# Flags of the first pair in two steps, and PSUM evacuations moved from VectorE to ScalarE, in a fused chunk-selecting attention and mixture-of-experts kernel

## The chip, the cores and the metric

The kernel runs on one core of a Trainium2 chip. The metric is the device time in microseconds of one execution; the time before is the median of 3 runs. All positions in the trace are microseconds from the start of the profiled span, which is 256.9 us long.

## The reference, cut to what matters

The first half is attention over 4 batches of 8 heads, 768 positions and head size 64. Keys are grouped in 24 chunks of 32. For every query an upper bound of its score with each chunk is formed, the six best chunks within the causal range are kept, and a softmax over the kept, causal keys gives the output.

```python
k_min = np.min(k_chunks, axis=3); k_max = np.max(k_chunks, axis=3)
ub = np.sum(np.maximum(q[:, :, :, None, :] * k_min[:, :, None, :, :],
                       q[:, :, :, None, :] * k_max[:, :, None, :, :]), axis=-1)
top_chunks = np.argsort(np.where(causal, ub, -1e9), axis=-1)[..., -top_k:]
scores = np.where(sel & (pos[:, None] >= pos[None, :]), scale * q @ k.T, -1e9)
x = softmax(scores) @ v
```

The second half takes the 3072 rows of x (512 wide) through a dense two-layer network with a relu and adds the output of one of eight experts, chosen per row by the largest of eight gate logits and scaled by its softmax probability.

## The kernel before, in words

The 32 heads are worked on as 16 **pairs** of heads (`NP`), four pairs to a batch (`HP`). A pair goes through three stages.

*Preparation* of pair p. GpSimd casts k and q to fp16 (`cast_qk`, L468 and L470). `prep_k` transposes k on TensorE into PSUM (L481), ScalarE copies it out as `kp` (L483), VectorE reduces it to chunk minima and maxima (L497 to L501). `prep_q` transposes q (L513); ScalarE takes its relu `qp` (L516) and VectorE its negative (L517). `prep_kt` copies the two heads' keys into the stationary operands `kT` (L505, L506). `prep_ub` forms the upper bounds in one PSUM tile on TensorE (L523, L527); VectorE finds the eight largest of each row block with ten MAX8 instructions (L533) and compares all bounds with the sixth (L535), which gives the **flags**: 1 for a chunk that is not kept. `prep_s` transposes the six blocks of flags (L541) into a PSUM tile and copies it into rows 64 to 127 of `r0` (L544, VectorE) and rows 0 to 63 of `r1` (L545, ScalarE for the first pair, VectorE for the others). r0 and r1 are the moving operands of the two heads: 64 rows of q and 64 rows of flags.

`expand(i)` writes, on ScalarE, the large constant that multiplies the flags into `kT` buffer i (L144, L145), so that scores of dropped chunks vanish in the exponential. There are three such buffers, used in turn, and each is filled once.

*Scores and values.* A pair's work is cut into 11 **units** of 3 or 4 blocks of 128 by 128. `scores(p, u)` multiplies kT by r0 or r1 (L554), ScalarE takes the exponential `ex` (L558), GpSimd clears what lies above the diagonal in the units that hold diagonal blocks (L560), `av` multiplies by the values (L573), and `norm` (L582, L584) divides into x, held for a whole batch in `xbig`. The first unit needs only columns 0 to 511 of r0; the second needs columns up to 639.

*Fills.* While the pairs of batches 1 to 3 run, the dense network, the gate and the routing of the batch before are slipped in between the units. They begin with `xtr`: six blocks of x are transposed (L257) and copied out as `xT` (L258, VectorE). All fills share one PSUM bank while attention runs. The fills of the last batch, and the experts' 28 blocks of rows, come after the attention.

Instructions are traced in the order of the functions at the end of the kernel, but an engine's queue does not follow it: the program's builder places on each engine what is ready first, and trace order decides among what is ready together. `tc.issue_after(x)` puts what is traced inside it, as far as it runs on x's engine, behind x in that engine's queue; it is no wait for x's result. The main loop runs two units ahead (`ahead_n`) with `scores`, and puts the flags' transposes of pair p+1 into unit 2 of pair p and the preparation of pair p+2 into units 4 to 9.

Of the kernel before, what the change touches and what calls it, by code (L numbers as in the profile page):

```python
# [11 lines left out]
AF = mybir.ActivationFunctionType  # L12
ALU = mybir.AluOpType
# [4 lines left out]
def kernel(  # L18
# [12 lines left out]
    nc = tc.nc  # L31
    B, H, S, D = q.shape
    NT = S // 128
    NC = S // 32
# [6 lines left out]
    HP = H // 2  # L41
    NP = B * HP
# [34 lines left out]
    st = [dict() for _ in range(NP)]  # L77

    def load(p, names="kqv"):
        if p >= NP:  # L80
            return
        b, hp = divmod(p, HP)
        for nm, src in (("k", k), ("q", q), ("v", v)):
            if nm not in names:
                continue
            f = aload.tile([128, 2, NT, D], FP, name=nm + "f")
            st[p][nm] = f
            for g in range(2):
# [9 lines left out]
    ident = const.tile([128, 128], HF)  # L98
# [44 lines left out]
    def expand(i):  # L143
        nc.scalar.copy(kT[i][0][64:96, :], exf[0:32])  # L144
        nc.scalar.copy(kT[i][1][0:32, :], exf[0:32])  # L145
# [74 lines left out]
    NU = len(units)  # L220
# [18 lines left out]
    latest = {}  # L239
# [8 lines left out]
    def batch_fills(b):  # L248
# [4 lines left out]
        def xtr(mi):  # L253
            def f():
                tp = ptile("tr", [128, NK, 128], HF, "tp")
                for ko in range(NK):
                    nc.tensor.transpose(tp[:, ko], xbig[b % 2][:, mi, ko * 128 : (ko + 1) * 128], ident)  # L257
                nc.vector.tensor_copy(xT[:, :, mi * 128 : (mi + 1) * 128], tp)  # L258
            return f

        def gate():
# [193 lines left out]
    with (  # L455
# [21 lines left out]
        def prep_k(p):  # L477
            s = st[p]
            pk = pprep.tile([128, S], HF, name="pp")
            for t in range(NT):  # L480
                nc.tensor.transpose(pk[:, t * 128 : (t + 1) * 128], s["k16"][:, t].rearrange("p g d -> p (g d)"), ident)  # L481
            s["kp"] = kp = ahead.tile([128, S], HF, name="kp")
            nc.scalar.copy(kp.rearrange("d (T p j) -> d T p j", p=128, j=NJ),  # L483
                           pk.rearrange("d (T j p) -> d T p j", p=128, j=NJ))
            ks = ahead.tile([128, 2, NC], HF, name="ks")
            if p == 0:

                pc = pk.rearrange("d (T j c w) -> d T c j w", j=NJ, c=8, w=16)
                for i, op in enumerate((ALU.max, ALU.min)):
                    nc.vector.tensor_reduce(out=ks[:, i].rearrange("d (T c) -> d T c", c=8), in_=pc, op=op,  # L490
                                            axis=mybir.AxisListType.XY)
            else:
                kc = kp.rearrange("d (c w) -> d c w", w=32)
                k1 = ahead.tile([128, 2, NC, 16], HF, name="k1")
                k2 = ahead.tile([128, 2, NC, 8], HF, name="k2")
                for i, op in enumerate((ALU.max, ALU.min)):
                    nc.vector.tensor_tensor(k1[:, i], kc[:, :, 0:16], kc[:, :, 16:32], op)  # L497
                    nc.vector.tensor_tensor(k2[:, i], k1[:, i, :, 0:8], k1[:, i, :, 8:16], op)
                    nc.vector.tensor_reduce(out=ks[:, i], in_=k2[:, i], op=op, axis=mybir.AxisListType.X)
            s["kb"] = kb = ahead.tile([128, 2, 2, NC], HF, name="kb")  # L500
            nc.vector.tensor_tensor(kb, ks.unsqueeze(2).to_broadcast([128, 2, 2, NC]), hmask, ALU.mult)  # L501

        def prep_kt(p):
            kp = st[p]["kp"]
            nc.vector.tensor_copy(kT[p % NB][0][0:64], kp[0:64])  # L505
            nc.vector.tensor_copy(kT[p % NB][1][64:128], kp[64:128])  # L506

        def prep_q(p):
# [7 lines left out]
            nc.scalar.activation(qp, pq, AF.Relu)  # L516
            nc.vector.tensor_single_scalar(r0, pq, -1.0, ALU.mult)  # L517

        def prep_ub(p):

            s = st[p]
            ub = pprep.tile([128, NT, 2, NC], FP, name="pp")
            nc.tensor.matmul(ub.rearrange("p t g c -> p (t g c)"), ident, cbias.rearrange("p t g c -> p (t g c)"),  # L523
                             start=True, stop=False, skip_group_check=True)
            for t in range(NT):
                for n, (src, j) in enumerate(((s["qp"], 0), (s["qp"], 1), (rT[p % NB][0], 1))):
                    nc.tensor.matmul(ub[:, t].rearrange("p g c -> p (g c)"), src[:, t * 128 : (t + 1) * 128],  # L527
                                     s["kb"][:, j].rearrange("p g c -> p (g c)"),
                                     start=False, stop=(n == 2), skip_group_check=True)
            m = m8[p % 2]  # L530
            for t in range(1, NT):
                for g in range(2):
                    nc.vector.max(out=m[:, t, g], in_=ub[:, t, g, 0 : 4 * t + 4])  # L533
            flags = fl[p % 2].rearrange("p t (g c) -> p t g c", g=2)[:, :, :, 0:NC]
            nc.vector.tensor_tensor(flags, ub, m[:, :, :, 5:6].to_broadcast([128, NT, 2, NC]), ALU.is_lt)  # L535

        def prep_s(p):
            s = st[p]
            ps = pprep.tile([128, S], HF, name="pp")
            for t in range(NT):  # L540
                nc.tensor.transpose(ps[:, t * 128 : (t + 1) * 128], fl[p % 2][:, t], ident)  # L541
            r0, r1 = rT[p % NB]
            nc.vector.tensor_copy(r1[64:128], r0[64:128])
            nc.vector.tensor_copy(r0[64:128], ps[64:128])  # L544
            (nc.scalar.copy if p == 0 else nc.vector.tensor_copy)(r1[0:64], ps[0:64])  # L545

        def scores(p, u):
            s = st[p]
            pc = units[u]
            sp = psc.tile([128, 512], FP, name="sp")  # L550
            o = 0
            for g, kt, a, z in pc:
                w = (z - a) * 128
                nc.tensor.matmul(sp[:, o : o + w], kT[p % NB][g][:, kt * 128 : (kt + 1) * 128],  # L554
                                 rT[p % NB][g][:, a * 128 : z * 128], start=(o == 0), stop=True, skip_group_check=True)
                o += w
            ex = aexp.tile([128, 512], HF, name="ex")
            nc.scalar.activation(ex[:, 0:o], sp[:, 0:o], AF.Exp, scale=-0.125)  # L558
            if pc[0][1] == pc[0][2]:
                latest["pool"] = nc.gpsimd.affine_select(out=ex, in_=ex, compare_op=ALU.is_ge, fill=0.0, base=0,  # L560
                                        pattern=[[0, 4], [1, 2], [2, 64]], channel_multiplier=-1)
            s["ex", u] = ex
# [38 lines left out]
        load(2, "v")  # L601
        load(3, "v")
        prep_s(0)
        prep_k(1)
        prep_q(1)
        prep_kt(1)
        cast_qk(2)
        load(4, "kq")
        expand(1)
        prep_ub(1)  # L610
        expand(2)

        wq = [(e, w) for e in range(E) for w in range(2)]
        ahead_n = 2
        LAG = 1

        def finish(p, u):
# [6 lines left out]
                    fills.clear()  # L624
                    fills.update(batch_fills(p // HP)[-1])

        seq = [(p, u) for p in range(NP) for u in range(NU)]
        for i in range(ahead_n):
            scores(*seq[i])
# [176 lines left out]
```

## Time and profile before

| | |
|---|---|
| time, median of 3 (range) | 266.76 us (265.68 to 266.89) |
| profiled span | 256.9 us |
| busy: TensorE, VectorE, ScalarE, GpSimd | 83%, 70%, 69%, 63% of the span |
| batch 0, first exponential to flags of pair 5 | 16.5 to 54.5 us |
| batches 1 to 3 of the attention | 54.5 to about 168 us |
| last dense fills and experts | about 168 to 257 us |
| one exponential of 128x512, mean | 612 ns, 144 of them |
| one copy of 64x768 flags out of PSUM: VectorE, ScalarE | 548 ns, 792 ns |
| one copy of 128x512 `xT` out of PSUM, VectorE | 416 ns, 24 of them |

The shares of the whole span are averages over three stages with different limits, so the stages have to be read one by one. A mean duration is that of one instruction [...]; on ScalarE and VectorE the next instruction may start before that, so the distance from start to start in a row of back-to-back instructions is the price that a queue pays. The row of L558, for instance, has 4 instructions in 1.96 us, 0.49 us for each.

### The profile page before, as it was taken

How to read it: one execution, taken by the hardware profiler on the slowest of the kernel's cores; microseconds unless marked ns; L12 is line 12 of the kernel's file. 1: busy time of each engine (PE TensorE's matmuls, PEld its weight loads, DVE VectorE, ACT ScalarE, POOL GpSimd, SP SyncE). 2: the span in 40 equal slices, each digit the busy share in tenths (PEclk: the TensorE clock that was granted, in tenths of full speed). 3: DMA queues.
4: the chain of work that ended last, by engine and by line, in shares of the span. 5: the costliest groups of instructions: out<-in, count | busy, mean ns of one | idle time of the engine just before them, and what ended most of it. 6: DMA issues, size and time to landing. Idle time of an engine off the chain costs nothing. (4 is left out here: it accounts for less than half of the span.)

```text
span 256.9 us, 7296 instructions
## 1 busy us (share of the span) xinstructions
PE 214.5 (83%) x2547; PEld 142.1 (55%) x2547; DVE 180.5 (70%) x617; ACT 178.5 (69%) x332; POOL 160.7 (63%) x197
## 2 busy tenths in 40 slices
PE   1388887796899798899986899979999999999960
PEld 0256566565666477656665666646555555455520
DVE  6868899999968789986799997237633344455440
ACT  2698888887679887778897877954666554555530
POOL 3746988766468475867866553510887453887671
PEclk9999999999999999999999999999999999999995
DMA  6999999999959999999999884265499999786885
GB/s 174 261 266 239 199 219 262 210 188 217 281 128 240 237 215 202 183 304 174 281 228 234 159 172 129 83 187 158 106 302 137 252 276 236 115 142 84 108 103 77
DMA packets 75109, 49.89 MB, mean 194 GB/s; under 512 B 29632, under 2 KB 68160, under 8 KB 75072
## 3 DMA queue, kind: packets, MB, share of 16 engines
q0 software_dynamic: 15216, 19.09, 46.4%
q1 hardware_dynamic: 59856, 30.33, 46.1%
q8 instruction: 21, 0.34, 0.5%
q14 instruction: 16, 0.13, 0.2%
HBM read 41.66 MB, written 18.23 MB: 233 GB/s over the span
## 5 line engine op out<-in xcount | busy, mean ns | idle before, releaser
L558 ACT ACTIVATE ex<-sp 128x512 f16<-128x512 f32 (+1 forms) x176 | 92.4, 593 | 11.1 <-PE sp L554 10.8
L554 PE MATMUL sp<-rT,kT 128*128 128x128 f16 (+3 forms) x384 | 63.2, 261 | 2.6 <-ACT ex L558 1.1
L720 POOL DMA_INDIRECT out_dram<-yo,xg x28 | 43.7, 1561 | 20.7 <-DVE yo L719 14.3
L560 POOL TENSOR_SCALAR_AFFINE_SELECT ex<-ex 128x512 f16<-128x512 f16 x48 | 32.6, 689 | 37.4 <-ACT ex L558 35.1
L573 PE MATMUL op<-v,ex 128*128 128x65 f16 x672 | 49.5, 194 | 4.4 <-POOL ex L560 2.9
L573 PEld LDWEIGHTS <-ex 128*128 128x128 f16 x672 | 37.3, 98 | 18.2 <-POOL ex L560 6.7
L368 POOL DMA_INDIRECT table<-xbig,slot x24 | 24.4, 1019 | 19.1 <-DVE nf L324 11.3
L719 DVE TENSOR_SCALAR yo<-yp,xg 128x512 f32<-128x512 f32 x28 | 21.0, 750 | 21.6 <-PE yp L716 18.6
L554 PEld LDWEIGHTS <-kT 128*128 128x128 f16 x384 | 28.3, 98 | 6.4 <-issue 4.1
L710 ACT COPY ehT<-tp 128x512 f16<-128x512 f16 x28 | 16.4, 585 | 20.5 <-PE tp L708 20.4
L699 PE MATMUL hp<-we,exT 128*128 x112 | 29.1, 379 | 1.1 <-DVE xbig L584 1.1
L716 PE MATMUL yp<-we,ehT 128*128 x112 | 28.7, 379 | 0.8 <-ACT ehT L710 0.8
L383 PE MATMUL hp<-xT,wd 128*128 128x384 f16 x128 | 26.2, 325 | 1.7 <-ACT hT L385 1.1
L392 PE MATMUL yp<-wd,hT 128*128 128x512 f16 x96 | 24.4, 379 | 0.9 <-ACT ys L395 0.4
L702 ACT ACTIVATE eh<-hp 128x512 f16<-128x512 f32 x28 | 16.7, 597 | 11.5 <-PE hp L699 11.5
L693 DVE COPY exT<-tp 128x512 f16<-128x512 f16 x28 | 11.9, 423 | 15.1 <-PE tp L691 14.3
L395 ACT COPY ys<-yp 128x512 f32<-128x512 f32 x24 | 14.3, 594 | 9.6 <-PE yp L392 6.8
L385 ACT ACTIVATE hT<-hp 128x384 f16<-128x384 f32 x32 | 15.9, 496 | 6.8 <-PE hp L383 6.5
L497 DVE TENSOR_TENSOR k<-kp 128x384 f16<-128x384 f16 x30 | 13.3, 479 | 9.1 <-ACT kp L483 9.1
L584 DVE TENSOR_TENSOR xbig<-op,rs 128x384 f16<-128x384 f32 x32 | 17.6, 550 | 0.4
L483 ACT COPY kp<-pp 128x768 f16<-128x768 f16 x16 | 12.9, 805 | 6.4 <-PE pp L481 6.4
L475 POOL CAST v<-vf 128x768 f16<-128x768 f32 x16 | 13.6, 853 | 5.3 <-DMA vf<-in_v_dram 3.3
(126 smaller groups left out, 403.1 us busy)
## 6 DMA issues: line engine op xcount, KB each, us to landing
we<-in_moe_w_dram POOLq DMA_DIRECT2D x16, 512.0 KB, 8.0
kf<-in_k_dram SPq DMA_DIRECT2D x32, 192.0 KB
qf<-in_q_dram SPq DMA_DIRECT2D x32, 192.0 KB
vf<-in_v_dram SPq DMA_DIRECT2D x32, 192.0 KB
out_dram<-ys SPq DMA_DIRECT2D x48, 128.0 KB
xg<-table SPq DMA_DIRECT2D x28, 136.0 KB
table<-zt SPq DMA_DIRECT2D x9, 136.0 KB
wd<-in_moe_w_dense_dram POOLq DMA_DIRECT2D x2, 512.0 KB
```

Source lines behind the costliest of these rows:

```text
L368: sc = nc.gpsimd.indirect_dma_start(out=table, out_offset=bass.IndirectOffsetOnAxis(ap=keep["slot"][:, t : t + 1], axis=0), in_=xbig[b % 2 ...
L383: nc.tensor.matmul(hp, wd[:, ko, j * 128 : (j + 1) * 128], xT[:, ko, g * G * 128 : (g + 1) * G * 128], start=(ko == 0), stop=(ko == NK - 1))
L392: nc.tensor.matmul(yp, hold["h"][:, j, i * 128 : (i + 1) * 128], wd[:, NK + j], start=(j == 0), stop=(j == NK - 1))
L554: nc.tensor.matmul(sp[:, o : o + w], kT[p % NB][g][:, kt * 128 : (kt + 1) * 128], rT[p % NB][g][:, a * 128 : z * 128], start=(o == 0), sto ...
L558: nc.scalar.activation(ex[:, 0:o], sp[:, 0:o], AF.Exp, scale=-0.125)
L560: latest["pool"] = nc.gpsimd.affine_select(out=ex, in_=ex, compare_op=ALU.is_ge, fill=0.0, base=0, pattern=[[0, 4], [1, 2], [2, 64]], chan ...
L573: nc.tensor.matmul(s["op", g][:, t * (D + 1) : (t + 1) * (D + 1)], ex[:, o : o + 128], v16[p % NB][:, g, kt, :], start=first, stop=(last_o ...
L584: nc.vector.tensor_tensor(xbig[b % 2][:, :, h0 : h0 + D], opv[:, :, 0:D], rs.to_broadcast([128, NT, D]), ALU.mult)
L699: nc.tensor.matmul(hp, s["xT"][:, ko], wef[:, bass.ds(offs[i] + ko * 512, 512)], start=(ko == 0), stop=(ko == NK - 1))
L716: nc.tensor.matmul(yp, s["hT"][:, j], wef[:, bass.ds(offs[i] + (NK + j) * 512, 512)], start=(j == 0), stop=(j == NK - 1))
L719: nc.vector.tensor_scalar(o, yp, s["x"][:, Dm : Dm + 2].bitcast(FP), None, ALU.mult)
L720: sc = nc.gpsimd.indirect_dma_start(out=out, out_offset=bass.IndirectOffsetOnAxis(ap=s["x"][:, Dm + 2 : Dm + 4].bitcast(mybir.dt.int32), a ...
```

## The change

It has three parts. The first pair's flags are made in two steps, blocks 0 to 3 and blocks 4 and 5, so that the first unit can begin with the first step; the two units of scores that the loop runs ahead are traced before the preparation of pair 1, and the ScalarE instructions of that preparation, with the constants of `kT` buffers 1 and 2, are queued behind the second exponential. ScalarE copies the lower half of the flags (r1) out for pairs 1 to 4 as well as for pair 0. And ScalarE copies three of the six `xT` blocks of the first three batches. The aim is to have the first exponential sooner, and to share PSUM evacuation[...].

```diff
@@ xtr
-                nc.vector.tensor_copy(xT[:, :, mi * 128 : (mi + 1) * 128], tp)
+                evac = nc.scalar.copy if b < B - 1 and mi % 2 else nc.vector.tensor_copy
+                evac(xT[:, :, mi * 128 : (mi + 1) * 128], tp)
@@ prep_ub
-            m = m8[p % 2]
-            for t in range(1, NT):
+            s["ub"] = ub
+            for a, z in steps(p):
+                select(p, a, z)
+
+        def steps(p):
+
+            return ((0, 4), (4, NT)) if p == 0 else ((0, NT),)
+
+        def select(p, a, z):
+            ub, m = st[p]["ub"], m8[p % 2]
+            for t in range(max(a, 1), z):
                 for g in range(2):
                     nc.vector.max(out=m[:, t, g], in_=ub[:, t, g, 0 : 4 * t + 4])
-            flags = fl[p % 2].rearrange("p t (g c) -> p t g c", g=2)[:, :, :, 0:NC]
-            nc.vector.tensor_tensor(flags, ub, m[:, :, :, 5:6].to_broadcast([128, NT, 2, NC]), ALU.is_lt)
+            flags = fl[p % 2].rearrange("p t (g c) -> p t g c", g=2)[:, a:z, :, 0:NC]
+            nc.vector.tensor_tensor(flags, ub[:, a:z], m[:, a:z, :, 5:6].to_broadcast([128, z - a, 2, NC]), ALU.is_lt)
@@ prep_s
-            for t in range(NT):
-                nc.tensor.transpose(ps[:, t * 128 : (t + 1) * 128], fl[p % 2][:, t], ident)
             r0, r1 = rT[p % NB]
             nc.vector.tensor_copy(r1[64:128], r0[64:128])
-            nc.vector.tensor_copy(r0[64:128], ps[64:128])
-            (nc.scalar.copy if p == 0 else nc.vector.tensor_copy)(r1[0:64], ps[0:64])
+            for a, z in steps(p):
+                for t in range(a, z):
+                    nc.tensor.transpose(ps[:, t * 128 : (t + 1) * 128], fl[p % 2][:, t], ident)
+                cols = slice(a * 128, z * 128)
+                nc.vector.tensor_copy(r0[64:128, cols], ps[64:128, cols])
+
+                (nc.scalar.copy if p <= HP else nc.vector.tensor_copy)(r1[0:64, cols], ps[0:64, cols])
@@ the order of the first pairs
         prep_s(0)
-        prep_k(1)
-        prep_q(1)
-        prep_kt(1)
-        cast_qk(2)
-        load(4, "kq")
-        expand(1)
-        prep_ub(1)
-        expand(2)
+        seq = [(p, u) for p in range(NP) for u in range(NU)]
+        ahead_n = 2
+        for i in range(ahead_n):
+            scores(*seq[i])
+        with tc.issue_after(latest["exp"].ins):
+            prep_k(1)
+            prep_q(1)
+            prep_kt(1)
+            cast_qk(2)
+            load(4, "kq")
+            expand(1)
+            prep_ub(1)
+            expand(2)
```

`latest["exp"]` is the exponential that `scores` issued last. The two scores that stood ahead of the main loop are gone from there.

More of the change, by code (lines that the diff above doesn't have):

```diff
@@ L529, in prep_ub @@
                                      start=False, stop=(n == 2), skip_group_check=True)
-            m = m8[p % 2]
-            for t in range(1, NT):
+            s["ub"] = ub
[6 more added lines that the diff above has]
+            for t in range(max(a, 1), z):
                 for g in range(2):
                     nc.vector.max(out=m[:, t, g], in_=ub[:, t, g, 0 : 4 * t + 4])
-            flags = fl[p % 2].rearrange("p t (g c) -> p t g c", g=2)[:, :, :, 0:NC]
-            nc.vector.tensor_tensor(flags, ub, m[:, :, :, 5:6].to_broadcast([128, NT, 2, NC]), ALU.is_lt)
+            flags = fl[p % 2].rearrange("p t (g c) -> p t g c", g=2)[:, a:z, :, 0:NC]
+            nc.vector.tensor_tensor(flags, ub[:, a:z], m[:, a:z, :, 5:6].to_broadcast([128, z - a, 2, NC]), ALU.is_lt)
         def prep_s(p):
-            s = st[p]
             ps = pprep.tile([128, S], HF, name="pp")
-            for t in range(NT):
-                nc.tensor.transpose(ps[:, t * 128 : (t + 1) * 128], fl[p % 2][:, t], ident)
             r0, r1 = rT[p % NB]
             nc.vector.tensor_copy(r1[64:128], r0[64:128])
-            nc.vector.tensor_copy(r0[64:128], ps[64:128])
-            (nc.scalar.copy if p == 0 else nc.vector.tensor_copy)(r1[0:64], ps[0:64])
+            for a, z in steps(p):
[4 more added lines that the diff above has]
+                (nc.scalar.copy if p <= HP else nc.vector.tensor_copy)(r1[0:64, cols], ps[0:64, cols])
         def scores(p, u):
@@ L557, in scores @@
             ex = aexp.tile([128, 512], HF, name="ex")
-            nc.scalar.activation(ex[:, 0:o], sp[:, 0:o], AF.Exp, scale=-0.125)
+            latest["exp"] = nc.scalar.activation(ex[:, 0:o], sp[:, 0:o], AF.Exp, scale=-0.125)
             if pc[0][1] == pc[0][2]:
@@ L603 @@
         prep_s(0)
-        prep_k(1)
-        prep_q(1)
-        prep_kt(1)
-        cast_qk(2)
-        load(4, "kq")
-        expand(1)
-        prep_ub(1)
-        expand(2)
+        seq = [(p, u) for p in range(NP) for u in range(NU)]
[11 more added lines that the diff above has]
+            expand(2)
         wq = [(e, w) for e in range(E) for w in range(2)]
-        ahead_n = 2
         LAG = 1
@@ L625, in finish @@
                     fills.update(batch_fills(p // HP)[-1])
-        seq = [(p, u) for p in range(NP) for u in range(NU)]
-        for i in range(ahead_n):
-            scores(*seq[i])
         for i, (p, u) in enumerate(seq):
```

## The prediction

> **What bounds the kernel now.** The chain that ended last is of no use here: it ends in one scatter and goes no further back. So I cut the span into stages and read the busy time of each engine by stage; the cuts are the starts of the flags' transposes (L541), one for each pair. Columns: length, then busy time and number of instructions of PE, PEld, DVE, ACT, POOL, the clock, DMA share and GB/s.
>
> ```profile
> 14.88:22.30 7.42, 6.73 (x77) 4.23 (x75) 5.47 (x25) 6.85 (x14) 3.71 (x6) 1.00 1.24 254
> 22.30:30.30 8.00, 6.47 (x102) 4.62 (x102) 7.54 (x27) 7.07 (x14) 6.79 (x10) 1.00 1.06 225
> 30.30:37.90 7.60, 6.32 (x104) 4.85 (x105) 6.93 (x28) 6.43 (x13) 6.51 (x22) 1.00 1.15 194
> 37.90:46.50 8.60, 6.44 (x109) 4.97 (x108) 8.31 (x29) 7.32 (x15) 7.35 (x12) 1.00 1.19 259
> 46.50:54.50 8.00, 7.03 (x128) 5.46 (x128) 7.50 (x31) 7.35 (x15) 5.82 (x9) 1.00 0.94 173
> ```
>
> The first row is pair 0: ScalarE is the fullest engine, 6.85 of 7.42 us. In the four rows after it VectorE is, with 7.54 + 6.93 + 8.31 + 7.50 = 30.28 of 32.2 us, or 94%; ScalarE follows with 28.17. The same view of the first ten microseconds of batches 1, 2 and 3, where the transposes of x fall:
>
> ```profile
> 54.50:65.20 10.70, 7.60 (x138) 5.89 (x135) 10.12 (x39) 7.42 (x15) 5.89 (x8) 1.00 1.14 230
> 94.00:104.00 10.00, 8.73 (x169) 7.38 (x167) 9.38 (x32) 8.36 (x18) 5.99 (x9) 1.00 0.96 188
> 134.00:144.00 10.00, 7.48 (x133) 6.22 (x132) 9.73 (x34) 7.38 (x15) 6.00 (x9) 1.00 1.17 236
> ```
>
> VectorE is 94 to 97% busy in each head, TensorE and ScalarE have 1.3 to 3.3 us of idle time. Who waits there is in the waits of 54 to 66 us (total, times, longest):
>
> ```profile
> POOL ex L560 <- ACT ex L558: 4.0, 3, 2.1
> ACT ex L558 <- PE sp L554: 1.7, 4, 0.8
> ...
> PE tp L257 <- DVE xT L258: 0.7, 1, 0.7
> ```
>
> GpSimd waits for exponentials, ScalarE for scores, TensorE for an evacuation by VectorE: the waits lead back to VectorE. Later in each batch (104 to 134 us) TensorE is at 88 to 94% and no engine stands out, and from 175 to 215 us TensorE is busy for 39.61 of 40 us. That last stage holds none of the changed instructions, so what the attention gains or loses should reach the end one to one.
>
> DMA is busy throughout, but after 22 us no cast of k or q waits for a load, and the one long wait for values (L475, 2.2 us) ends at 20.08. I take no load as the limit.
>
> The opening, on ScalarE's timeline (start, duration):
>
> ```profile
> 11.49 0.83 ACT L144 COPY kT<-exf 32x768 f16<-32x768 f16 x1
> 12.35 0.83 ACT L145 COPY kT<-exf 32x768 f16<-32x768 f16 x1
> 13.20 0.83 ACT L144 COPY kT<-exf 32x768 f16<-32x768 f16 x1
> 14.05 0.83 ACT L145 COPY kT<-exf 32x768 f16<-32x768 f16 x1
> 15.16 0.80 ACT L483 COPY kp<-pp 128x768 f16<-128x768 f16 x1 [0.27 <-PE pp L481]
> 15.85 0.79 ACT L545 COPY rT<-pp 64x768 f16<-64x768 f16 x1
> 16.54 0.60 ACT L558 ACTIVATE ex<-sp 128x512 f16<-128x512 f32 x1
> 17.24 0.81 ACT L516 ACTIVATE qp<-pp 128x768 f16<-128x768 f16 x1
> 17.95 1.96 ACT L558 ACTIVATE ex<-sp 128x512 f16<-128x512 f32 x4
> ```
>
> The four copies of the constant (buffers 1 and 2) run from 11.49 to 14.88, while nothing else is ready: they cost nothing. Then ScalarE is busy nearly without a gap until 22.65; the third exponential starts at 17.95 + 0.49 = 18.44, the first of pair 1 at about 24.3 (the second instruction of a row at 23.84).
>
> [...]
>
> **Part 1, the opening.** Ten MAX8 take 0.95 us from 12.19, the compare 0.46. Six tenths of the first and four sixths of the second give 0.57 + 0.31: first flags at 13.07 in place of 13.60. Four transposes instead of six (0.82 for six at the start of the kernel) take some 0.6, r0's columns 0 to 511 some 0.40 (560 ns for 768), scores 0.5: first exponential at about 14.9, 1.6 us sooner than 16.54. The second step (0.37 for four MAX8, 0.16 compare) is hidden beside these transposes[...]: second exponential at about 15.8, sooner by 2.1.
>
> Against that, the four constant copies lose their free place. They are queued behind the second exponential, are ready at once, and are traced before the third exponential. kp and the relu stood ahead of the third before, too. So after the second exponential (ends 16.3) come kp 0.69, relu 0.69 and four copies at 0.86 from start to start, 3.44: third exponential at 16.3 + 4.8 = 21.1, later by 2.7 than 18.44. Pair 0 was ScalarE's stage, so I count 2.7 us as loss there, between 0.9 (one buffer's two copies first, the others in gaps) and 3.4 (all four unhidden). VectorE, which waits 0.9 us for kp now, gets it at 17.0 instead of 15.9, but has slack of 2 us in pair 0.
>
> **Part 2, flags of pairs 1 to 4.** Four VectorE copies go: 0.57 each from start to start (23.40 to 23.97), 2.3 us. VectorE falls from 30.28 to 28.0 in the four rows. ScalarE gets four at 0.69 (15.85 to 16.54), 2.8: 28.17 + 2.8 = 30.9 by busy time. But [...] there are about five rows in a pair, so packed it is 30.9 - 4 x 0.5 = 28.9. ScalarE becomes the fuller engine by a little. At 96% filled the four pairs take 28.9 / 0.96 = 30.1 instead of 32.2: gain 2.1 us. Bounds: no gain at 90%, 3.3 at 100%. Nothing new waits for this copy but the units of head 1, the last five and a half of a pair; the exponentials queued behind it wait 0.69.
>
> **Part 3, transposes of x.** In each head VectorE loses three copies at 0.33 from start to start (59.38 to 59.71), 1.0 us; ScalarE gets three. No row shows ScalarE copying this shape from PSUM in the attention, but the experts' L710 has it at 585 ns, and the equal-sized exponential gives 0.49 in a row: 1.5 us, in a stage where ScalarE has 1.6 to 3.3 idle. VectorE stays the fullest (10.12 - 1.0 = 9.1 against 7.42 + 1.5 = 8.9 in the first). I take 0.87 of the 1.0, since ScalarE's queue can hold a copy behind an exponential and the single fill bank then stays occupied: 2.6 us for three heads, between 1.2 and 3.0.
>
> **Sum.** +2.7 - 2.1 - 2.6 = -2.0: 266.76 - 2.0 = **264.8 us**.
>
> **Rivals.**
> *ScalarE becomes the limit.* For it: it is the fullest in pair 0, and gets 3.4 + 2.8 us more in the first 40. Against it: its idle time before each row. The constants cost 3.4, batch 0 gains nothing, the heads 1.2 because copies wait behind exponentials: +2.2, 269.0 us.
> *The constants hide after all.* They are pushed between exponentials that wait for scores, and pairs 1 to 4 make up the rest. Then 0 - 2.1 - 3.0 = -5.1: 261.7 us. For it: 4.0 us of ScalarE idle in the four rows of batch 0. Against it: these gaps lie at the ends of rows, under a microsecond each.
> *All cancels.* The heads are held by the single fill bank and by scores, so that they give 1.2; the opening's 2.7 is met by 2.1: -0.6, 266.2 us. For it: TensorE at 71 to 87% in the heads.
>
> **How the numbers follow.** Forecast 0.44, constants hidden 0.20, all cancels 0.14, ScalarE the limit 0.22. The bound of 0.5% is 1.33 us, so faster is below 265.4: about three quarters of the first case with its spread of 1 us (0.35) and all of the second, and a little of the third: 0.57. Slower is above 268.1: nearly all of the last case, 0.21. The rest, 0.22, is the same. The range reaches near both outer cases: 261.4 to 268.6.
>
> **What would show it.** First exponential near 14.9; L144 and L145 in front of the third exponential, which starts near 21; pair periods of 7.5 us in batch 0 with ScalarE above 93%; heads shorter by 0.9 each with VectorE still above 90%; the last stage unchanged. The prediction is wrong if the constants land elsewhere in ScalarE's queue, if another order of the fills costs more than the evacuations save, or if flags on ScalarE delay the scores of head 1.

## The result, and the profile after

The changed kernel takes 279.02 us (median of 4 runs, 277.34 to 281.72) against 266.82 us for the kernel before on the same chip. The ratio is 1.044, with a 95% interval of 1.037 to 1.051: slower by 4.4%, or 12.2 us, where 2 us less were forecast. From chip to chip the kernel before takes 258.9 to 266.8 us, so every ratio below is to its own runs on the chip of that experiment. Times are medians of all runs; some executions are slow whatever the kernel, and the ratios and their intervals leave those out.

The same view by stages as in the prediction, of the changed kernel (length, then busy time and number of instructions of PE, PEld, DVE, ACT, POOL, then the clock, DMA share, GB/s). The cuts are again the starts of the flags' transposes, now L553; the first row begins at 15.60, within pair 0:

```profile
15.60:23.50 7.90, 4.27 (x52) 3.38 (x52) 5.26 (x23) 7.29 (x12) 1.86 (x3) 0.84 1.28 255
23.50:31.90 8.40, 7.68 (x107) 6.28 (x106) 6.07 (x27) 7.29 (x15) 4.63 (x7) 0.75 0.53 125
31.90:42.70 10.80, 7.53 (x109) 5.83 (x106) 8.70 (x28) 7.58 (x15) 7.06 (x12) 0.84 1.11 190
42.70:54.70 12.00, 8.57 (x110) 6.49 (x108) 9.58 (x27) 8.40 (x16) 8.02 (x24) 0.73 0.83 177
54.70:62.80 8.10, 6.50 (x105) 4.96 (x103) 6.91 (x27) 7.10 (x15) 5.11 (x7) 0.98 1.05 207
```

Before, the four rows of pairs 1 to 4 were 8.00, 7.60, 8.60 and 8.00 us. Now they are 8.40, 10.80, 12.00 and 8.10. ScalarE was to be above 93% in them: it is at 70% in the two longest. VectorE is at 80%. No engine is full, so the rows have become a chain of waits. VectorE even has *more* busy time in the third and fourth rows (8.70 and 9.58 us) than before (6.93 and 8.31), though a copy a pair was taken from it: its instructions last longer (two `k<-k` 2.29 us in place of 0.42, in the next section).

The heads of batches 1 to 3:

```profile
62.80:72.80 10.00, 9.28 (x172) 7.57 (x169) 9.08 (x33) 9.62 (x21) 6.63 (x10) 1.00 1.03 195
106.00:116.00 10.00, 8.40 (x162) 7.19 (x160) 8.96 (x33) 8.56 (x17) 4.59 (x7) 1.00 0.94 197
149.30:159.30 10.00, 8.18 (x154) 6.85 (x155) 8.70 (x32) 7.91 (x16) 5.13 (x8) 1.00 0.81 163
```

VectorE has come down to 87 to 91%, as it was meant to. ScalarE's timeline of the opening (start, duration):

```profile
14.72 0.60 ACT L570 ACTIVATE ex<-sp 128x512 f16<-128x512 f32 x1
15.87 0.36 ACT L557 COPY rT<-pp 64x256 f16<-64x256 f16 x1 [0.55 <-DVE rT L555]
16.52 0.60 ACT L570 ACTIVATE ex<-sp 128x512 f16<-128x512 f32 x1 [0.28 <-PE sp L566]
17.01 0.79 ACT L484 COPY kp<-pp 128x768 f16<-128x768 f16 x1
17.69 0.83 ACT L517 ACTIVATE qp<-pp 128x768 f16<-128x768 f16 x1
18.54 0.83 ACT L144 COPY kT<-exf 32x768 f16<-32x768 f16 x1
...
21.07 0.83 ACT L145 COPY kT<-exf 32x768 f16<-32x768 f16 x1
21.80 2.56 ACT L570 ACTIVATE ex<-sp 128x512 f16<-128x512 f32 x5
```

The opening went nearly as forecast: first exponential at 14.72 (forecast 14.9), the four constants ahead of the third, which starts at 21.80 (forecast 21.1). What the forecast did not follow stands in the fourth row: kp of pair 1, at 17.01 in place of 15.16.

The waits of 31.9 to 54.8 us, the two long rows:

```profile
ACT ex L570 <- PE sp L566: 6.0, 4, 2.5
PE pp L528 <- DVE kb L502: 4.9, 2, 2.8
```

Before, 30.3 to 46.5 us had 2.1 and 1.2 us for these two (L558 for scores, L527 for `kb`). ScalarE now waits for scores, and scores stand in TensorE's queue behind the bounds of the next pair, which wait for `kb`, the end of VectorE's reduction of k.

Where the time lies along the kernel, read from the last `norm` of each batch in the traces (another profiled run of the kernel before has the same ends to within 0.2 us):

| length of batch, us | 0 (from the start) | 1 | 2 | 3 | end of attention |
|---|---|---|---|---|---|
| before | 52.6 | 41.7 | 42.2 | 36.3 | 172.8 |
| after | 62.8 | 43.4 | 43.5 | 39.4 | 189.1 |
| difference | +10.2 | +1.7 | +1.3 | +3.1 | +16.3 |

The profiled run of before was on a faster chip than its timed ones (258.92 us), and the stage after the attention takes 82.5 to 89.2 us in the traces, depending on the chip and the kernel; so ends of attention are compared between traces, and times only between runs of one chip. The attention itself seems not to depend on the chip: on one where the kernel before takes 264.77 us, batches 0 and 1 of `xT` alone took 52.4 and 41.7 us, and batches 2 and 3 of the flags alone 42.2 and 36.5, which is what they take before. What the attention lost did not come back in full as time (16.3 against 12.2 us), so the prediction's "one to one" did not hold; that difference was not followed up.

### The profile page after: what moved, and what is told of

Its sections match the earlier page's. It is cut to its first block, busy times and chain, and to the rows that moved or that the text cites. A ratio compares the mean times of both kernels' runs of the same rounds, so it can differ in the third digit from the quotient of the medians.

```text
span 275.5 us, 7295 instructions
## 1 busy us (share of the span) xinstructions
PE 220.6 (80%) x2547; PEld 147.2 (53%) x2547; DVE 184.1 (67%) x606; ACT 185.1 (67%) x346; POOL 161.8 (59%) x197
## 3 DMA queue, kind: packets, MB, share of 16 engines
q0 software_dynamic: 15216, 19.09, 43.5%
## 5 line engine op out<-in xcount | busy, mean ns | idle before, releaser
L570 ACT ACTIVATE ex<-sp 128x512 f16<-128x512 f32 (+1 forms) x176 | 94.4, 597 | 13.6 <-PE sp L566 12.0
L566 PE MATMUL sp<-rT,kT 128*128 128x128 f16 (+3 forms) x384 | 68.4, 272 | 2.4 <-ACT ex L570 1.4
L585 PE MATMUL op<-v,ex 128*128 128x65 f16 x672 | 53.9, 199 | 1.9 <-POOL ex L572 1.5
L585 PEld LDWEIGHTS <-ex 128*128 128x128 f16 x672 | 40.8, 102 | 15.3 <-POOL ex L572 3.2
L369 POOL DMA_INDIRECT table<-xbig,slot x24 | 25.0, 1040 | 21.3 <-DVE nf L325 11.3
L566 PEld LDWEIGHTS <-kT 128*128 128x128 f16 x384 | 29.6, 102 | 5.7 <-issue 3.4
L723 ACT COPY ehT<-tp 128x512 f16<-128x512 f16 x28 | 16.4, 585 | 22.1 <-PE tp L721 16.9
L498 DVE TENSOR_TENSOR k<-kp 128x384 f16<-128x384 f16 x30 | 19.8, 696 | 12.7 <-ACT kp L484 12.7
L715 ACT ACTIVATE eh<-hp 128x512 f16<-128x512 f32 x28 | 16.7, 597 | 11.3 <-PE hp L712 10.4
L528 PE MATMUL pp<-kb,qp 128*128 128x48 f16 x192 | 11.6, 189 | 11.8 <-DVE kb L502 9.3
L706 DVE COPY exT<-tp 128x512 f16<-128x512 f16 x28 | 11.8, 422 | 12.0 <-PE tp L704 8.7
L528 PEld LDWEIGHTS <-qp 128*128 128x128 f16 x192 | 10.4, 100 | 14.0 <-issue 12.2
```

Source lines behind the costliest of these rows:

```text
L369: sc = nc.gpsimd.indirect_dma_start(out=table, out_offset=bass.IndirectOffsetOnAxis(ap=keep["slot"][:, t : t + 1], axis=0), in_=xbig[b % 2 ...
L570: latest["exp"] = nc.scalar.activation(ex[:, 0:o], sp[:, 0:o], AF.Exp, scale=-0.125)
L585: nc.tensor.matmul(s["op", g][:, t * (D + 1) : (t + 1) * (D + 1)], ex[:, o : o + 128], v16[p % NB][:, g, kt, :], start=first, stop=(last_o ...
```

## What changed besides the instructions: two things that the traces show

**The preparation moved to another place in the queues.** Ordering each kernel's ScalarE queue in the trace, I counted how many exponentials of pair p-2 stand ahead of `kp` of pair p. Before, it is 10 or 11, that is all of them or all but one, for pairs 2 to 7, 11 and 15, and 7 for the others. After, it is 7 for every pair. The diff says nothing of these pairs: the builder places what is ready first, so an order can move far from an edit. By parts, the opening alone has 7, 9 and 9 for pairs 2 to 4 and the old order behind them, `xT` alone has 7 for pairs 11 and 15, and the flags alone keep the old order to within one place.

**In the new place it meets GpSimd's casts.** VectorE's timeline of pair 3's preparation, changed kernel:

```profile
33.67 1.26 DVE L498 TENSOR_TENSOR k<-kp 128x384 f16<-128x384 f16 x2 [0.63 <-ACT kp L484]
34.85 2.29 DVE L499 TENSOR_TENSOR k<-k 128x192 f16<-128x192 f16 x2
```

GpSimd's in the same stretch, and TensorE's next instruction after its matmuls at 35.01:

```profile
34.01 1.45 POOL L572 TENSOR_SCALAR_AFFINE_SELECT ex<-ex 128x512 f16<-128x512 f16 x2
35.42 0.81 POOL L469 CAST k<-kf 128x768 f16<-128x768 f32 x1
36.19 0.85 POOL L471 CAST q<-qf 128x768 f16<-128x768 f32 x1
```

```profile
38.10 0.24 PE L528 MATMUL pp<-kb,qp 128*128 128x48 f16 x2 [2.81 <-DVE kb L502]
```

The two L499 take 0.42 us for pair 1, where GpSimd is idle. Here they take 2.29, until the second cast is over, and TensorE stands for 2.81 us. The same happens for pair 4: 2.90 us, from 45.58 to 48.48, with the casts from 46.79 to 48.37. One of pair 4's two L499 alone takes 2.27 us, from within a select to the end of the second cast, so it was held over a row of GpSimd's instructions and not over one. Not every instruction is held: `tensor_reduce` between them (L500, 30 times) never took longer than 0.35 us in any of the runs, and VectorE's copies of flags out of PSUM (L555, L557) never longer than 0.56 us in the changed kernel. The traces show these times; by what VectorE is held was not shown.

To compare kernels I add up VectorE's busy time, over all pairs, of the instructions of a pair's preparation that read and write SBUF alone, without `tensor_reduce`: `k`, `kb`, and the copies `kT<-kp` and `rT<-rT`. Call it the **SBUF work**. Before it is 53.2 us (53.6 in the other profiled run), after 62.3, for the same instructions.

## The experiments

All ratios are to the kernel before on the same chip.

| kernel | time, us | ratio, 95% interval | end of attention, us | SBUF work, us |
|---|---|---|---|---|
| changed | 279.02 | 1.044 (1.037 to 1.051) | 189.1 | 62.3 |
| opening alone | 270.76 | 1.022 (1.016 to 1.027) | 180.2 | 57.3 |
| flags of pairs 1 to 4 alone | 267.62 | 1.011 (1.008 to 1.014) | 176.7 | 57.0 |
| `xT` alone | 268.23 | 1.013 (1.007 to 1.019) | 177.0 | 56.6 |
| flags and `xT` | 272.57 | 1.031 (1.023 to 1.038) | 182.6 | 63.0 |
| opening alone, constants early | 266.16 | 1.010 (1.007 to 1.013) | 176.8 | 55.5 |
| changed, constants early | 267.82 | 1.031 (1.024 to 1.038) | 182.9 | 64.5 |
| changed, casts later | 271.56 | 1.032 (1.025 to 1.039) | 182.4 | 49.6 |
| before, casts later | 261.68 | 1.010 (1.005 to 1.015) | 175.5 | 54.1 |
| `xT` alone, casts later from pair 5 | 263.20 | 1.016 (1.010 to 1.022) | 176.7 | 51.2 |

And with work left out, so that these are not candidates but measurements:

| kernel, casts and loads of k and q left out from pair 3 on | time, us | ratio, 95% interval | end of attention, us | SBUF work, us |
|---|---|---|---|---|
| before | 252.28 | 0.972 (0.962 to 0.982) | 166.2 | 46.2 |
| changed | 257.65 | 0.993 (0.990 to 0.995) | 171.8 | 46.8 |
| flags and `xT` | 256.93 | 0.989 (0.982 to 0.996) | 170.6 | 49.6 |
| `xT` alone | 253.85 | 0.980 (0.976 to 0.985) | 168.1 | 48.2 |

### The three parts one by one

Opening alone (the hunks of `prep_ub`, `prep_s` and the order of the first pairs, with `p == 0` kept for ScalarE's copy and VectorE for `xT`):

> The opening alone (part 1), flags and x copies on VectorE as before. Phase theory: the queue order has 7, 9, 9, 11 exponentials ahead of kp of pairs 2 to 5, so only the first one or two pairs meet the casts; the opening's 2 to 3 us and one collision of 2 us: 269 to 273 us. ScalarE theory: only the opening's own delay, 1.2 to 1.7 us at the flags of pairs 1 and 2: 268 to 269 us. If the opening alone is the loss: 276 us or more.

Flags alone, the kernel before with one line:

```diff
-            (nc.scalar.copy if p == 0 else nc.vector.tensor_copy)(r1[0:64], ps[0:64])
+            (nc.scalar.copy if p <= HP else nc.vector.tensor_copy)(r1[0:64], ps[0:64])
```

> Part 2 alone, the flags of pairs 1 to 4 on ScalarE. Phase theory: the order stays as in the kernel before (10 or 11 exponentials ahead of kp), so no more collisions and no idle TensorE; the prediction's sum says up to 2 us faster: 264 to 267 us. ScalarE theory: ScalarE at 28.9 of 30 us holds back exponentials in batch 0: 268 to 271 us.

`xT` alone, the kernel before with the hunk of `xtr`:

> Part 3 alone, three of six x copies on ScalarE. Phase theory: the heads of the batches get shorter by 1 us or more each, but ScalarE's queue now has 7 exponentials ahead of kp for all pairs from 8 on (pair 11 and pair 15 had 11), so the pairs after a head meet the casts more often; gain and loss nearly cancel: 265 to 270 us, with batch 0 unchanged. The prediction's sum: 264.2 us. ScalarE theory: heads not shorter, since copies wait behind exponentials: 267 to 268 us.

Flags and `xT` together:

> Parts 2 and 3 without the opening (flags in one step, constants in their free place, pair 1 prepared before the first scores). Phase theory: the loss comes from the order that the opening sets, in which the chunk reduction of pair p+2 on VectorE runs beside GpSimd's casts of k and q in batch 0; here ScalarE's queue has 10 or 11 exponentials of pair p ahead of kp of pair p+2 up to pair 7, as in the kernel before, so batch 0 keeps its time (flags of pair 5 within 1.5 us of 54.5) and the whole is 266 to 272 us. ScalarE theory: the copies given to ScalarE are the loss; then this is about as slow as the changed kernel, 276 to 279 us.

Each part by itself makes the kernel slower: by 2.2, 1.1 and 1.3%, which add up to 4.5, the loss of the whole (4.4). No part alone brings a gain, and none of the three was worth what it was costed at. They lose in different places. The opening costs 7.3 us in batch 0 (59.9 against 52.6), gives 1.7 back in batch 1 and costs 1.6 in batch 2; the flags 2.4 in batch 0 and 1.3 in batch 1; `xT` nothing in batches 0 and 1, 1.3 in batch 2 and 3.1 in batch 3.

The idea that was called phase theory, that the loss comes from the order that the opening sets, failed on the flags. Alone they keep that order, and with `xT` they keep it in batch 0, each to within one place; yet the flags of pair 5 come at 57.6 and 58.3 us in place of 54.5, and both times are just above the range that this idea gave. So batch 0 can lose time without the preparation moving.

### What the flags' copy did for VectorE

One place, around pair 2's flags, shows what became of the time of the copy that was taken from VectorE. VectorE in the kernel before:

```profile
30.83 0.56 DVE L544 COPY rT<-pp 64x768 f16<-64x768 f16 x1 [0.60 <-PE pp L541]
31.42 0.55 DVE L545 COPY rT<-pp 64x768 f16<-64x768 f16 x1
31.89 0.18 DVE L582 RECIPROCAL rs<-op 128x6 f32<-128x6 f32 x1
31.99 0.63 DVE L497 TENSOR_TENSOR k<-kp 128x384 f16<-128x384 f16 x2
```

and GpSimd:

```profile
30.15 0.83 POOL L468 CAST k<-kf 128x768 f16<-128x768 f32 x1
30.91 0.83 POOL L470 CAST q<-qf 128x768 f16<-128x768 f32 x1
```

While GpSimd casts (30.15 to 31.74), VectorE copies flags out of PSUM, and starts on k when the casts are over. With the copy gone (flags alone), VectorE and GpSimd:

```profile
29.99 0.56 DVE L544 COPY rT<-pp 64x768 f16<-64x768 f16 x1 [0.60 <-PE pp L541]
31.15 1.76 DVE L497 TENSOR_TENSOR k<-kp 128x384 f16<-128x384 f16 x2 [0.60 <-ACT kp L483]
```

```profile
30.97 0.83 POOL L468 CAST k<-kf 128x768 f16<-128x768 f32 x1
31.73 0.97 POOL L470 CAST q<-qf 128x768 f16<-128x768 f32 x1
```

k starts 0.84 us sooner, falls onto the casts and takes 1.76 us in place of 0.63: it ends at 32.91, where it ended at 32.62 before. Here the saved 0.57 us of VectorE became a wait for GpSimd. Besides, ScalarE's copy stands in its queue until VectorE is done with the same PSUM tile, and the exponentials behind it wait too. ScalarE at pair 3's flags, flags alone:

```profile
41.15 0.79 ACT L545 COPY rT<-pp 64x768 f16<-64x768 f16 x1 [1.03 <-DVE rT L544]
```

The two copies of one tile ran at the same time in none of the traces (in the changed kernel ScalarE's starts 0.03 to 0.83 us after the end of VectorE's), so an engine was changed and nothing was made parallel. That the casts are all of this part's loss is not shown: with casts and loads of k and q left out (below), flags and `xT` together are still 0.9 points slower than `xT` alone, though these two intervals overlap.

### The constants' place

In the opening alone, and then in the changed kernel, the four constant copies are traced ahead of the first scores:

```diff
+        expand(1)
+        expand(2)
         for i in range(ahead_n):
             scores(*seq[i])
...
-            expand(1)
             prep_ub(1)
-            expand(2)
```

> The opening alone, but with the four constant copies traced in front of the first scores, so that they keep their free place on ScalarE; flags and x copies on VectorE. ScalarE's queue then has 11 exponentials ahead of kp for pairs 2 to 7, as in the kernel before. If the constants are what makes the opening slow: 263 to 266 us against 270.8 with them queued behind the second exponential. If the split of the flags or the scores ahead of pair 1's preparation is what costs: 269 to 271 us.

> The changed kernel with the four constant copies traced ahead of the first scores, so that they have their free place again. The same edit brought the opening alone from 1.022 to 1.010. If the losses add up, this takes 1.044 - 0.012 = about 1.03; if the misplaced constants only start a delay that the later collisions would bring anyway, it stays at 1.04.

The misplaced constants cost 1.2 to 1.3% (1.022 to 1.010, and 1.044 to 1.031), some 3.3 us: close to the 3.44 us that they occupy ScalarE, and somewhat more than the 2.7 of the forecast. That it is the copies' own time is not shown: with them early, the opening alone also has the old order again (11 exponentials ahead of `kp` for pairs 2 to 7), and TensorE's clock is full from 19.8 us on and not from 26.8 (see the last section). With them early, the changed kernel takes as long as flags and `xT` alone, so there the rest of the opening costs nothing. But the opening alone still loses 1.0% with its constants free and its first exponential at 14.69. Its ScalarE queue (opening alone, constants early) shows why:

```profile
14.69 0.58 ACT L569 ACTIVATE ex<-sp 128x512 f16<-128x512 f32 x1
...
16.29 0.60 ACT L569 ACTIVATE ex<-sp 128x512 f16<-128x512 f32 x1 [0.28 <-PE sp L565]
16.78 0.79 ACT L483 COPY kp<-pp 128x768 f16<-128x768 f16 x1
```

kp of pair 1 is still behind the second exponential, 1.6 us later than before, and the flags of pair 1 come at 23.6 in place of 22.3. Pair 1 can't begin without them, so the first exponential's 1.8 us are lost again at the first change of pairs.

### Are the casts the cause?

First by leaving work out of the changed kernel and of the kernel before, the casts alone:

> The changed kernel without the casts of k and q from pair 3 on: those pairs use pair 2's k and q, so half of GpSimd's casts are left out; the order on TensorE and ScalarE is that of the changed kernel. Contention theory (VectorE's chunk reduction [...] is held while GpSimd casts): the reduction takes 1.2 us for every pair, the gaps of 2 to 3 us on TensorE in batch 0 and the halved clock go; 265 to 270 us, within 3 or 4 us of the kernel before without these casts. ScalarE theory (evacuations and constants on ScalarE hold exponentials back whatever GpSimd does): 276 us or more, and the distance stays at 10 us or more.

> The same omission (casts of k and q from pair 3 on) in the kernel before, as the reference for the run above. Contention theory: its reduction is held for some 5 us in all now (23.9 us of VectorE time for 15 pairs against 18 without), part of it beside other work: 260 to 264 us. ScalarE theory: 264 to 266 us, no change, since no ScalarE instruction is touched.

The changed kernel took 266.23 us, 1.007 (1.004 to 1.010), and the kernel before 265.27, 0.999 (0.994 to 1.003), so the gap nearly closed. But this pair is not a clean measurement: without casts the loads of k and q run ahead and those of v come late (in the kernel before, GpSimd waits 12.1 us for values in the profile without the casts, 3.3 with them). So the loads went too:

```diff
     def load(p, names="kqv"):
-        if p >= NP:
+        if p >= NP or names == "kq" and p > 2:
@@ cast_qk
+            if p > 2:
+                s["k16"], s["q16"] = st[p - 1]["k16"], st[p - 1]["q16"]
+                return
```

> The kernel before without the casts and without the loads of k and q from pair 3 on (those pairs use pair 2's), because leaving out the casts alone let these loads run ahead and made the values late. Contention theory: the chunk reduction takes 18 to 20 us in all instead of 23.9, values are no longer late, 258 to 263 us. ScalarE theory: 263 to 265 us.

> The changed kernel with the same omissions (no casts and no loads of k and q from pair 3 on); orders on TensorE and ScalarE as in the changed kernel. Contention theory: what is left of the 12 us is the opening's own delay, 1 to 4 us above the kernel before with the same omissions: 260 to 266 us. ScalarE theory: still 10 us or more above it.

> Parts 2 and 3 without the opening, with the same omissions. Contention theory: the two parts' gains, which the prediction put at 2.1 and 2.6 us, come out once no cast stands against VectorE: 1 to 5 us faster than the kernel before with the same omissions. ScalarE theory: as with all work kept, 8 us slower than it.

> Part 3 alone, with the casts and loads of k and q left out from pair 3 on (later pairs use pair 2's data). The kernel before with the same left out took 0.972 of before (252.3 us), parts 2 and 3 together 0.989. If part 3 lost only by collisions, this takes 0.972 or less. If something else in it costs time, the longer last batch above all, it takes 0.98 to 0.99, and batch 3 is longer by 1.5 to 2 us than in the kernel before with the same left out.

The kernel before gets 2.8% faster, the changed one by 5.1 points (1.044 to 0.993). The difference between the two falls from 12.2 us to 257.65 - 252.28 = 5.4, and the SBUF work of the two is nearly the same (46.2 and 46.8 us). So roughly half of the loss needs GpSimd's casts of k and q (or their loads, which this edit can't tell apart), and some 5 us do not; by the intervals of the two ratios the share is known only roughly.

The forecasts of the contention theory were too high for both kernels, and for flags and `xT` its forecast failed outright. They were to be 1 to 5 us faster than the kernel before with the same left out, and are 4.7 us slower; with all work kept it is 7.8. So the gains that the prediction saw in parts 2 and 3 did not lie hidden behind these casts. GpSimd's selects and its casts of v are still there, and flags and `xT` have 3.4 us more SBUF work than before even here (49.6 against 46.2), so collisions with those are not excluded. What holds the rest was not settled.

Then with all work kept, by moving the casts two units:

```diff
-            if u == 7:
+            if u == 9:
                 with tc.issue_after(latest["pool"].ins):
                     cast_qk(p + 3)
```

> The changed kernel with all work kept, but the casts of k and q traced at unit 9 instead of 7 of a pair, which puts them behind the select of the next pair's first unit in GpSimd's queue; the order on ScalarE (7 exponentials ahead of kp) stays. Contention theory: in batch 0 the casts now come after the chunk reduction, which falls from 3.7 and 4.2 us for pairs 3 and 4 to about 1.3; 267 to 273 us. ScalarE theory: 277 to 280 us, nothing else is changed. If later casts make k late: more than 280 us.

> The kernel before, with all its work, and only the casts of k and q moved from unit 9's place after unit 7 to after unit 9. Here the chain over k of most pairs runs after the last units of a pair, not in the middle. If the cause is the overlap of these casts with that chain, the same move that made the changed kernel 7 us faster must here be of no use or harmful: the chain's four instructions, 23.9 us over 15 pairs, grow to 27 or more, and the time goes up by 1 to 2%. If a later cast is better in itself (loads further ahead, GpSimd's queue), this one gets faster by 1% or more.

The same edit takes 1.2 points off the changed kernel (1.044 to 1.032; the two intervals still overlap a little) and adds 1.0 to the kernel before. (The "7 us" in the second expectation was taken across two chips; by the ratios it is 3.2.) A later cast is thus not better in itself, which fits that it matters where the preparation stands. The direction was forecast, the victim was not. The chain over k did not grow in the kernel before; another instruction was hit. Before with later casts, VectorE and GpSimd:

```profile
114.63 3.24 DVE L543 COPY rT<-rT 64x768 f16<-64x768 f16 x1
```

```profile
115.29 0.84 POOL L468 CAST k<-kf 128x768 f16<-128x768 f32 x1
116.06 0.83 POOL L470 CAST q<-qf 128x768 f16<-128x768 f32 x1
116.83 0.83 POOL L475 CAST v<-vf 128x768 f16<-128x768 f32 x1
```

A copy from SBUF to SBUF, 0.36 us in the median, is held until three casts in a row are over, and TensorE then stands for 2.61 us from 116.8 on. The SBUF work hardly rose (53.2 to 54.1), so the sum does not tell the loss: what counts is which instruction is held, and who waits for it.

### Why the heads gained nothing

`xT` alone, with the casts moved from pair 5 on:

```diff
-            if u == 7:
+            if u == (9 if p >= 5 else 7):
```

> Part 3 alone, all work kept, with the casts of k and q after unit 9 in place of 7 from pair 5 on, where part 3 lets the chain over k run early. If collisions are what ate part 3's saving, the chain falls from 28.3 to about 24 us and the time from 1.013 to between 0.995 and 1.003 of before. If TensorE over a whole batch is the limit, the chain falls and the time stays at 1.008 or more.

The SBUF work fell by 5.4 us, below that of the kernel before, and the time stayed at 1.016. So collisions are not what ate part 3's saving, or later casts cost as much again: in this kernel, too, a copy (`kT<-kp`) is held for 3.19 us by three casts in a row, at 68.97. The runs without casts and loads are cleaner. The stages of batches 1, 2 and 3, first before, then `xT` alone:

```profile
52.90:92.60 39.70, 35.67 (x518) 25.86 (x519) 33.00 (x140) 33.28 (x66) 19.73 (x27) 1.00 0.74 150
92.60:130.40 37.80, 35.82 (x528) 26.30 (x525) 31.76 (x129) 33.77 (x68) 22.01 (x30) 1.00 0.88 165
130.40:166.20 35.80, 32.55 (x441) 22.62 (x437) 24.29 (x103) 29.19 (x60) 16.98 (x22) 1.00 0.75 167
```

```profile
52.40:92.00 39.60, 35.97 (x517) 26.04 (x518) 33.31 (x137) 34.28 (x69) 19.68 (x27) 1.00 0.73 152
92.00:130.40 38.40, 36.25 (x529) 26.23 (x525) 31.02 (x126) 35.07 (x71) 21.94 (x30) 1.00 0.85 164
130.40:168.10 37.70, 32.64 (x441) 22.62 (x436) 23.68 (x100) 30.55 (x63) 17.74 (x22) 1.00 0.71 157
```

Both end batch 2 at 130.4 us. TensorE is busy for 90, 95 and 91% of the three stages of the kernel before: over a whole batch it is the fullest engine, and shifting VectorE's copies to ScalarE takes nothing from it. That this is what holds a batch is argued from these shares and was not tested by itself. In the heads the saving is there. With all work kept, the pair periods of the heads fall from 10.7, 11.8 and 11.5 us to 10.2, 9.7 and 9.9. But the pairs after take it back: pairs 10 to 12 have 33.9 us in place of 30.1, and the last pair before pair 15's flags 12.7 in place of 10.4. Without casts and loads it is the same: pairs 10 to 12 have 29.9 us in place of 27.0. The fills are spread over a batch; what is done sooner in its head is waited for later.

Batch 3 is the one place where part 3 costs time without casts: 37.7 us against 35.8. Both have the same TensorE work there (32.64 and 32.55), and ScalarE has 1.4 us more of it. Most of the difference lies in pair 14 (13.0 us between the first exponentials of pairs 14 and 15, 10.4 before), in which pair 15 is prepared early and dense fills of batch 2 are still left. What exactly holds it there was not settled.

## Why the prediction was wrong, step by step

- **What bounds the kernel.** "VectorE is, with ... 94%" is right as busy time, and so is the reading of the heads. The step that failed is the next one, that freeing VectorE frees the pair. Where it was followed (pair 2), VectorE's busy time held work that *filled* the time of GpSimd's casts, and the instruction behind it then waited. The rows of GpSimd were read as a share (5.82 to 7.35 us of each row) and not for what is held beside them (k: 1.76 us, 0.63 when the casts are over). The casts are not the only reason: without them parts 2 and 3 are still 4.7 us slower, and that rest stays open.
- **Part 1** had the opening right: first exponential 14.72 (14.9), and the constants in the place named. The second exponential came at 16.52 and not 15.8. The second step's transposes (15.01) came behind the first step's copies (the last ends at 14.66), and five transposes of pair 1's k stood ahead of them too; which of the two they waited for was not shown. The size was not right: +2.7 us was forecast for the part and it costs 2.2%, 5.7 us. The constants' term was 3.3 instead of 2.7, if that is their own time. The rest goes back to the sentence "VectorE ... gets it at 17.0 instead of 15.9, but has slack of 2 us in pair 0". A delay of 1.1 us was forecast (it was 1.9: k starts at 17.84, 15.99 before) and costed at nothing. Slack in busy time is not slack on the chain from kp through k, `kb`, bounds and flags of pair 1. VectorE and then TensorE of the changed kernel:

```profile
17.84 0.63 DVE L498 TENSOR_TENSOR k<-kp 128x384 f16<-128x384 f16 x2 [2.00 <-ACT kp L484]
```

```profile
20.67 0.21 PE L528 MATMUL pp<-kb,qp 128*128 128x48 f16 x2 [2.33 <-DVE kb L502]
```

  VectorE idles 2.00 us for kp, TensorE 2.33 us for `kb`, and pair 1's flags come 1.2 us later (23.5 against 22.3) although pair 0 began 1.8 us sooner. In the changed kernel the preparation runs in the middle of each pair from there on, into the casts. TensorE's clock, of which the forecast says nothing, changed too.
- **Part 2** forecast -2.1 us; alone it costs 1.1%, 2.8 us. The working "packed it is ... 28.9" divided busy time by a share. (Its 0.5 us a pair is the author's estimate: five rows at 0.11 us, by which one exponential's 0.60 exceeds the 0.49 from start to start.) The pairs were held by an order (kp, k, `kb`, bounds), and the new copy put a wait into ScalarE's queue (1.03 us in the line above). The third doubt of the prediction's last part, "if flags on ScalarE delay the scores of head 1", comes near to this; how late head 1's scores came was not measured.
- **Part 3** forecast -2.6 us; alone it costs 1.3%, 3.4 us. The head periods did fall, by 4.2 us in sum, more than forecast. The step that failed counts a head's saving as the batch's: the prediction itself noted TensorE at 88 to 94% later in each batch and took that for a stage in which "no engine stands out" (from 104 to 114 us VectorE is in fact at 98%).
- **The sum.** The three losses measured alone add up, 5.7 + 2.8 + 3.4 = 11.9 us against 12.2. Part of that is chance, since not every combination does: with the constants early, the opening costs 1.0% alone and nothing on top of flags and `xT`.
- **The rivals.** "ScalarE becomes the limit" had the direction, but its mechanism did not happen: in the rows that lost most ScalarE is at 70%. The last stage was to stay as it was; from 191.3 to 231.3 us, as far behind the end of the attention as the prediction's 175 to 215, TensorE is busy for 37.49 of 40 us, 39.61 before. The warning that "another order of the fills costs more than the evacuations save" is nearest to what happened, but the order that moved is that of the preparations.

No version tried beats the kernel before with all its work done.

## What to carry to other kernels

Before moving work off a busy engine, ask what else runs while it is done: if the next instruction is held while that work lasts, as k was here beside GpSimd's casts (1.76 us against 0.63), the time saved turns into a wait. Follow a delayed result (here kp, 1.9 us late) along its chain to the next stage, not into the engine's idle time. And take the limit from the whole period in which work can move about (a batch), not from the stretch in which one engine is full.

## What the runs showed of the hardware

Two SBUF instructions of VectorE that take 0.42 us alone took up to 2.90 us beside GpSimd, and one copy of 0.36 us up to 3.24 us. GpSimd's casts of k and q kept 0.81 to 1.04 us in all runs but for one, so VectorE was nearly always the one that lost. In one place (changed kernel, 64.71) it was GpSimd, where a cast took 1.66 us beside VectorE instructions of their usual length.

TensorE's clock fell to half (0.50 granted, by its record in the trace) in three stretches of batch 0 of the changed kernel (from 20.9 for 6.8 us, from 38.0 for 3.4, from 48.2 for 6.8), each beginning in or right after a gap of 2.1 to 2.8 us. Not every gap of that length was followed by one: after 3.01 us (opening alone, before 48.61) the clock stood at full. What sets the clock and the lengths of these stretches was not shown.

In the opening alone the clock rises late. The six transposes of pair 1's flags, first before, then opening alone:

```profile
22.27 0.50 PE L541 MATMUL pp<-ident,fl 128*128 128x128 f16 x6
```

```profile
23.57 0.84 PE L552 MATMUL pp<-ident,fl 128*128 128x128 f16 x6
```

The second row is at half speed, 107 ns from one transpose to the next where the first has 56. By the clock's record in the traces, full speed starts at 18.5 us before and at 26.8 in the opening alone. The stage views hide this: they print 1.00 where the trace has no record of the clock yet.

How much of the loss is the clock's was not separated. It can't be all. In the opening alone `kp` of pair 3, which comes after the slow stretch, is 2.4 us late (33.52 against 31.16), and the other 4.9 of the 7.3 us of batch 0 are lost later, at full clock. In the changed kernel the second and third slow stretches, 10.2 us in all, lie in the two pairs that lost most, and there its share stays open. With casts and loads left out the clock of the changed kernel still fell twice (at 22.1 and 46.0, for 3.4 us each), so it may be part of the rest that the casts don't explain.
